# The seven column groups of the first batch, re-ordered: an FFT filter and a feed-forward block in one kernel

## The chip, the cores and the metric

The kernel runs on one core of one Trainium2 chip. Its engines are TensorE (PE in the profile, with its weight loads as PEld), VectorE (DVE), ScalarE (ACT), GpSimd (POOL) and SyncE (SP). SP, ACT and POOL each have a queue from which they issue transfers (DMAs); an issue that has to wait for data holds up everything behind it in that engine's queue. The metric is the device time of one execution in microseconds (us), lower is better.

## The reference

For each of 8 batches of 3008 rows by 256 columns, the rows are Fourier transformed, multiplied by a complex filter, and transformed back. The result goes through a feed-forward block of width 2048 with the activation h - tanh(h):

```python
X = np.fft.rfft(x, axis=1)
Y = X * (filt_r + 1j * filt_i)[None]
y = np.fft.irfft(Y, n=x.shape[1], axis=1)
h = y.reshape(-1, 256) @ w_in
out = (h - np.tanh(h)) @ w_out
```

Everything on TensorE is float32. The two weight matrices arrive as float64 and are converted to float32 on the chip.

## The kernel before, in words

The length 3008 is 64 times 47, and the transform is done in two steps each way. The first step (over 64) mixes the rows; the second (over 47, of which symmetry leaves 24) is done for 32 columns `a` of the first step. In batch 0 these 32 columns are worked in seven **column groups** (`SLOTS`): six of 5 columns, g = 0 to 5, with 5 times 24 = 120 partitions, and g = 6 with the last two columns, laid out at half width (two halves of 128 channels, one on top of the other).

The program has two parts. The **prologue** (from line 1101) works batch 0 up to the last step of its transform back; it also converts the first weights and takes the first columns of batch 1. The **main loop** (from line 1334) then runs over units `U`, four to each group of 4 output rows: `up` multiplies by w_in, `shrink` applies the activation, `down` multiplies by w_out, and the later batches' transforms are worked in between. The order of the instructions on each engine is the order in which the Python code emits them (`tc.manual_schedule()`): nothing reorders them.

In the prologue the loop over g (line 1208) emits for each group:

- `filters_of(g + 2)`, L1062: the filter rows of the group after next, loaded into one of three tiles, on SP for g above 1. Group 6 needs in addition a row that is zeroed (L1066), rows that `turned_rows` has brought into the DRAM tensor `filt` (read at L1067), and a shift of the upper half of the channels to the lower partitions by `under` (L1059, issue L1060);
- `across(g + 2)`, L1041: eight transposes on TensorE (L1050) and two copies by ACT into `a2`;
- `there0(g + 1)`, which is `forth`, L403: the second step of the transform for group g + 1. For each of two halves, two matmuls go to a bank (L411). ACT copies the first bank to `xy` (L414); VectorE forms sum and difference with the second (L416, L417) when the group's turn comes;
- `convert(3)`: three steps of the conversion of weights (`converted`, L169; ACT's step L180, VectorE's L182 to L200; seven steps a job, five jobs in the prologue). After the loop `convert(100)` does what is left;
- `filtered(g)`, L420: the complex product, L428 to L435 on VectorE and a last sum L437 on GpSimd, or on VectorE for g = 0, 5 and 6;
- `way_back()`: the transform back of the group before, `back0` (L1080): eight matmuls (L1087, L1089), two ACT copies (L1092) and two writes to the DRAM tensor `ct2` (L1093), on GpSimd's queue for g up to 4 and ACT's for g = 5. Group 6 has `back` (L446, L459).

`turned_rows` (L527) loads a filter row, negates it (L540), writes it to the DRAM tensor `less` (L541) and copies it turned round from there to `filt` (L531). The read waits for the write to land. Both are on GpSimd's queue, and in the loop they come at g = 2 in one piece, followed by the first two loads of the weights that the main loop converts (`begun`, L174).

After the loop, `rest` (L1073) reads the finished `ct2` back as `e2` in eight transfers on SP (L1077): four for the groups 0 to 4, and, behind the last way back, four for the groups 5 and 6. Then `first1` (L1170) takes the first eight columns of batch 1 (tile `x1`, loaded at g = 3; L1175), and `warmer(14)` (L1034) runs 14 matmuls whose result nobody reads. The main loop's first instruction on TensorE is `pu` (L576), which reads `e2`.

At the other end, `shrink` of the last unit but one ends with `combine` (L597 to L600: three differences and a fourth built on them) on VectorE, `down` of the last unit forms seven products (L787) and sums them (L801 to L821, two of the sums on GpSimd), and `store_last` (L877) transposes the result, copies it out of PSUM and sends it in two transfers, one each on SP and ACT.

The lists of steps that the two parts of the loop go by:

```python
steps_at = ([1, 1, 1, 1, 0, 1, 1, 0] if U > 1 else [0, 0, 1, 0, 2, 0, 2, 1])
...
chain = filtered(g, xy, fts.pop(g), V, V if g in (0, last_g - 1, last_g) else G, pro)
```

## Time and profile before

| | |
|---|---|
| runs, median (lowest to highest of 3) | 2564.8 us (2563.4 to 2569.96) |
| the profiled execution | 2566.24 us, span 2564.4 us |
| TensorE busy | 2540.9 us (99%) |
| VectorE busy | 1878.4 us (73%) |
| ScalarE busy | 1666.3 us (65%) |
| GpSimd busy | 1481.4 us (58%) |
| mean transfer rate | 83 GB/s, 212.43 MB in all |

The span is what the profiler saw between the first and the last instruction; the execution's own time is 1.8 us longer. All positions below are in microseconds from the span's start. A timeline row gives start, duration, engine, line, operation, what it writes and reads, its shape and how many instructions were merged into it, and in square brackets the idle time of the engine before it and what ended it. A float32 matmul stands in the trace as two records, so `x16` is eight matmuls. A row of the windows gives for each engine the busy time and the number of instructions in that stretch, then TensorE's granted clock (1.00 is full), the share of the DMA engines and what they moved. In a row of busy time and waits, the arrow `<-` ahead of an engine's name says what ended the wait.

### The profile page before, as it was taken

The page shows a single profiled execution, that of the slowest core. Times are in us where ns is not written, and L with a number is a line of the kernel's source. Part 1 is how long each engine was busy: PE and PEld are TensorE (multiplying, and loading weights), DVE is VectorE, ACT ScalarE, POOL GpSimd, SP SyncE. Part 2 cuts the span into 40 slices and gives each one's busy share as a digit, 9 for nine tenths or more (in the row PEclk, how much of TensorE's full clock was granted, in tenths as well). Part 3 has the DMA queues.
Part 4 walks back from the last instruction along what each step waited for, and adds up shares of the span by engine and source line. Part 5 has one row for each costly group of instructions (what it writes and reads, how often), then busy time and mean ns, then how long its engine had stood idle before and what let it go on. Part 6 is the DMA issues. An engine that isn't in the chain of part 4 may idle for free.

```text
span 2564.4 us, 44624 instructions
## 1 busy us (share of the span) xinstructions
PE 2540.9 (99%) x17076; PEld 2177.8 (85%) x17076; DVE 1878.4 (73%) x2265; ACT 1666.3 (65%) x2497; POOL 1481.4 (58%) x1124
## 2 busy tenths in 40 slices
PE   8999999999999999999999999999999999999998
PEld 7678888888898888988888888898889888898887
DVE  6788776887678876788668886688866877555555
ACT  4566666666666666666666666676666666666665
POOL 4256665666466655666656665566645666555552
PEclk9999999999999999999999999999999999999999
DMA  8873214422343323342233322443123322110110
GB/s 221 260 198 103 65 35 109 119 67 48 76 118 93 80 54 94 82 108 67 72 94 90 92 67 61 101 105 97 36 64 88 93 66 52 26 32 18 26 21 19
DMA packets 333660, 212.43 MB, mean 83 GB/s; under 512 B 231737, under 2 KB 304855, under 8 KB 329789
## 3 DMA queue, kind: packets, MB, share of 16 engines
q1 hardware_dynamic: 318511, 184.59, 29.5%
q0 software_dynamic: 11424, 17.03, 2.4%
q10 hardware_dynamic: 3502, 7.87, 0.9%
q8 instruction: 136, 2.23, 0.4%
q14 instruction: 87, 0.71, 0.1%
HBM read 128.75 MB, written 83.39 MB: 83 GB/s over the span
## 4 chain that ended last, share of the span: by engine, by line
PE 94%; DMA 2%; DVE 1%; ACT 1%; issue 1%; POOL 0%; ACTq 0%; POOLq 0%; DVEq 0%
PE o L787 43%; PE x L617 25%; PE z L617 12%; PE y L617 6%; PE pm L401 3%; PE pu L576 2%; DMA ct<-a 1%; PE pm L340 1%; DMA raw<-in_moe_w_in_dram 0%; DMA fh<-f 0%; DMA mats_sb<-mats 0%; PE pe L1089 0%; PE o L842 0%; PE pf L297 0%; PE warm L1038 0%
## 5 line engine op out<-in xcount | busy, mean ns | idle before, releaser
L787 PE MATMUL o<-t,wd 128*128 128x256 f32 (+1 forms) x3008 | 763.6, 377 | 0.0
L597 POOL TENSOR_TENSOR t<-h 128x512 f32<-128x512 f32 (+1 forms) x186 | 305.7, 1643 | 712.4 <-DVE h L739 703.9
L739 DVE TENSOR_TENSOR h<-h,y 128x1024 f32<-128x1024 f32 (+1 forms) x384 | 579.8, 1510 | 160.8 <-ACT y L735 157.3
L787 PEld LDWEIGHTS o<-t,wd 128*128 128x128 f32 x3008 | 569.3, 190 | 85.3 <-POOL o L815 15.1
L617 PE MATMUL x<-tu,wu 128*128 128x256 f32 (+1 forms) x2256 | 576.2, 378 | 0.2 <-ACT u L623 0.2
L787 PE MATMUL o<-h,wd 128*128 128x256 f32 (+1 forms) x2256 | 573.6, 377 | 1.8 <-DVE h L739 1.8
L787 PEld LDWEIGHTS o<-h,wd 128*128 128x128 f32 x2256 | 426.0, 190 | 72.8 <-issue 18.4
L623 ACT COPY s<-x 128x512 f32<-128x512 f32 (+1 forms) x188 | 108.6, 578 | 564.6 <-PE x L617 564.6
L617 PEld LDWEIGHTS x<-tu,wu 128*128 128x128 f32 x2256 | 423.6, 190 | 57.2 <-issue 3.7
L732 ACT ACTIVATE y<-y 128x1024 f32<-128x1024 f32 (+1 forms) x384 | 399.4, 1040 | 12.1
L735 ACT ACTIVATE y<-y 128x1024 f32<-128x1024 f32 (+1 forms) x384 | 399.8, 1041 | 4.6
L729 ACT ACTIVATE y<-h 128x1024 f32<-128x1024 f32 (+1 forms) x384 | 400.5, 1043 | 3.6 <-DVE h L665 1.7
L598 POOL TENSOR_TENSOR t<-h,t 128x512 f32<-128x512 f32 (+1 forms) x186 | 313.9, 1688 | 14.6
L600 POOL TENSOR_TENSOR t<-h,t 128x512 f32<-128x512 f32 (+1 forms) x186 | 303.7, 1633 | 0.0
L599 POOL TENSOR_TENSOR t<-h 128x512 f32<-128x512 f32 (+1 forms) x186 | 289.7, 1557 | 0.0
L623 ACT COPY u<-x 128x512 f32<-128x512 f32 (+1 forms) x376 | 213.3, 567 | 57.0 <-PE x L617 53.7
L665 DVE COPY h<-x 128x512 f32<-128x512 f32 (+1 forms) x188 | 127.8, 680 | 127.2 <-PE x L617 127.1
L617 PE MATMUL z<-tu,wu 128*128 128x256 f32 (+1 forms) x752 | 190.2, 376 | 0.4 <-DVE h L673 0.4
L617 PE MATMUL z<-ut,wu 128*128 128x256 f32 (+1 forms) x752 | 190.2, 376 | 0.4 <-DVE h L657 0.4
L617 PE MATMUL y<-ut,wu 128*128 128x256 f32 (+1 forms) x752 | 190.2, 376 | 0.0
L617 PE MATMUL x<-ut,wu 128*128 128x256 f32 (+1 forms) x752 | 190.2, 376 | 0.0
L657 DVE TENSOR_TENSOR h<-z,u 128x512 f32<-128x512 f32 (+1 forms) x188 | 127.2, 677 | 72.1 <-ACT u L623 71.1
(198 smaller groups left out, 2815.7 us busy)
## 6 DMA issues: line engine op xcount, KB each, us to landing
ft<-filt SPq DMA_DIRECT2D x28, 1024.0 KB
ct<-nn SPq DMA_DIRECT2D x56, 512.0 KB
e<-ct SPq DMA_DIRECT2D x47, 512.0 KB
a<-ct SPq DMA_DIRECT2D x112, 192.0 KB
out_dram<-ot SPq DMA_DIRECT2D x1248, 16.0 KB
x_sb<-in_x_dram SPq DMA_DIRECT2D x110, 128.0 KB
ct<-a SPq DMA_DIRECT2D x60, 128.0 KB
ct<-x_sb SPq DMA_DIRECT2D x60, 128.0 KB
```

The lines of the kernel that those rows point to most:

```text
L597: by.tensor_sub(t[0], b[0][1], b[0][0])
L598: by.tensor_sub(t[1], b[1][1], t[0])
L599: by.tensor_sub(t[2], b[1][1], b[0][1])
L600: by.tensor_sub(t[3], b[1][0], t[1])
L617: nc.tensor.matmul(bank[:, k], wu[:, q - 1, (2 * u + k) * 128:(2 * u + k + 1) * 128], rhs[q - 1], start=(first and k == 0), stop=True, ski ...
L623: ACT.copy(t, X)
L665: V.tensor_copy(h[:, 2, :, 0:w], X)
L729: ACT.activation(y[k], ht[k], AF.Arctan, scale=TURN)
L732: ACT.activation(y[k], y[k], AF.Tanh, scale=BEND)
L735: ACT.activation(y[k], y[k], AF.Square, scale=SCALE, accum_out=y_sums[:, 2 * U + k // 2:2 * U + k // 2 + 1])
L739: V.tensor_mul(ht[k], ht[k], y[k])
L787: nc.tensor.matmul(product(q), wd[:, q - 1, (2 * u + k) * 128: (2 * u + k + 1) * 128], rhs[q - 1][:, k], start=(u == 0 and k == 0 and q == ...
```

## The change

- `turned_rows`: the negation moves to GpSimd, and a `yield` splits the write to `less` from the copy that reads it. The write is emitted at g = 1, ahead of that group's way back, the copy at g = 2.
- The loads of the first two of the main loop's weights are emitted at g = 3 instead of g = 2, both on GpSimd's queue.
- `across(g + 2)` comes ahead of `filters_of(g + 2)`; group 6's zeroing moves from VectorE to GpSimd; the load of `x1` moves from g = 3 to the start of g = 2, and `first1` is made only where it is used.
- Group 5 (the sixth) forms its sums on TensorE: `forth(..., whole=True)` runs two matmuls into each result, so eight for four, and ACT copies both banks.
- Conversion steps in the loop: 3, 3, 3, 1, 0, 0 for g = 0 to 5, instead of 3 for each. From the third job on, the next job's ACT step is emitted after a job's third step.
- At g = 5 the way back of group 4 comes behind `there0(6)`, and no conversion stands there.
- The first four reads of `rest` go on GpSimd's queue.
- `warmer(14)` becomes `warmer(8)`.
- The tail: in the last unit but one a `yield` ahead of `combine`, and one more step at the end of `up`; the last `down` has its products in another order and one sum on VectorE instead of GpSimd; `store_last` works in two halves of two output columns each, with four transfers.

```diff
             for n, _ in enumerate(began[k]):
                 yield
-                if after and n == 2 and k + 1 < len(jobs):
+                if (after or k > 1) and n == 2 and k + 1 < len(jobs):
                     next(began[k + 1])
...
             for k in range(2):
-                nc.tensor.matmul(pa[:, k], way[2 * v + k], at[0:n, PLACE[2 * v + k], 0:w],
-                                 start=True, stop=True)
-            if v:
-                ACT.copy(xy[:, 2:4], pa)
+                if whole:
+                    nc.tensor.matmul(pa[:, k], way[k], at[0:n, PLACE[k], 0:w],
+                                     start=True, stop=False)
+                nc.tensor.matmul(pa[:, k], way[(3 - k if v else 2 + k) if whole else 2 * v + k],
+                                 at[0:n, PLACE[2 + k if whole else 2 * v + k], 0:w],
+                                 start=not whole, stop=True)
+            if v or whole:
+                ACT.copy(xy[:, 2 * v:2 * v + 2], pa)
             yield xy
-        V.tensor_add(xy[:, 0:2], pa, xy[:, 2:4])
-        V.tensor_sub(xy[:, 2:4], pa, xy[:, 2:4])
+        if not whole:
+            V.tensor_add(xy[:, 0:2], pa, xy[:, 2:4])
+            V.tensor_sub(xy[:, 2:4], pa, xy[:, 2:4])
...
-        V.tensor_scalar(out=t, in0=t, scalar1=-1.0, scalar2=None, op0=ALU.mult)
+        G.tensor_scalar(out=t, in0=t, scalar1=-1.0, scalar2=None, op0=ALU.mult)
         G.dma_start(dram(less_d, 0, [[DM, NH], [1, DM]]), t)
+        yield
         turned_to(1, less_d, NH - 1)
...
-        steps_at = ([1, 1, 1, 1, 0, 1, 1, 0] if U > 1 else [0, 0, 1, 0, 2, 0, 2, 1])
+        steps_at = ([1, 1, 1, 1, 0, 1, 1, 1] if U > 1 else [0, 0, 1, 0, 2, 0, 2, 1])
...
+        if U + 2 == 4 * len(groups):
+            yield
         combine(blocks, [t[:, k, :, 0:w] for k in range(4)],
...
-        mm(1, 2)
-        yield
-        if done:
+        last_unit = U + 1 == 4 * len(groups)
+        mm(*((2, 3) if last_unit else (1, 2)))
+        yield
+        if done and not last_unit:
             ACT.copy(p1, product(1))
             V.tensor_add(o[:, 0, 0:w], product(2), p1)
         yield
-        mm(3, 5)
-        yield
+        mm(*((1, 5) if last_unit else (3, 5)))
+        yield
+        if last_unit:
+            ACT.copy(p1, product(1))
+            V.tensor_add(o[:, 0, 0:w], product(2), p1)
...
-            G.tensor_add(x12, u2, x12)
+            (V if last_unit else G).tensor_add(x12, u2, x12)
+            if last_unit:
+                G.tensor_add(o[:, 1, w:2 * w], p1, p5)
...
-        for h, copy in ((0, ACT.copy), (1, V.tensor_copy)):
-            pt = psl([128, CH, 128], "xy"[h])
-            for j in range(CH):
-                nc.tensor.transpose(pt[:, j], o[:, h, j * 128:(j + 1) * 128], one)
-            copy(ot[:, :, h * 128:(h + 1) * 128], pt)
-        for (r, step, m, j, half), queue in zip(runs(c), (nc.sync, ACT)):
+        for lo, tag, copy in ((2, "x", ACT.copy), (0, "y", V.tensor_copy)):
+            pt = psl([128, 2, DM], tag)
+            for h in range(2):
+                for j in range(2):
+                    nc.tensor.transpose(pt[:, j, h * 128:(h + 1) * 128],
+                                        o[:, h, (lo + j) * 128:(lo + j + 1) * 128], one)
+            copy(ot[:, lo:lo + 2], pt)
...
                 if g == len(SLOTS) - 1:
-                    V.memset(t[0:1, 2:4], 0.0)
+                    G.memset(t[0:1, 2:4], 0.0)
...
             for g in range(last_g + 1):
+                if g == 2:
+                    x1 = load_x(big([128, 8, DM], F32, "x1"), 1, 0, 8)
                 if g + 2 <= last_g:
+                    a2[g + 2] = across(g + 2)
                     fts[g + 2] = filters_of(g + 2)
-                    a2[g + 2] = across(g + 2)
                 if g == 3:
                     e2s[0] = load_e2(0, 0, ())
-                    ones_1 = first1(load_x(big([128, 8, DM], F32, "x1"), 1, 0, 8))
                 if g == last_g - 1:
                     under(fts[last_g])
-                    convert(3)
-                    way_back()
                 if g < last_g:
                     there[g + 1] = there0(g + 1)
+                if g == last_g - 1:
+                    way_back()
                 next(there[g][0])
-                if g < last_g - 1:
-                    convert(3)
+                if g < last_g - 2:
+                    convert(3 if g < 3 else 1)
...
+                if g == 1:
+                    next(turning)
                 if g not in (0, last_g - 1):
                     way_back()
                 if g == 2:
                     next(turning)
+                if g == 3:
                     ahead = [begun(tiles1, job, queue=G) for job in jobs[5:7]]
-            rest(0, SG * (last_g - 1), [nc.sync])
+            rest(0, SG * (last_g - 1), [G])
...
-            warmer(14)
+            warmer(8)
```

More of the change, by code (lines that the diff above doesn't have):

```diff
@@ L401, in packed, with forth @@
             nc.tensor.matmul(to, weights_of, at, start=True, stop=True)
-    def forth(g, at, z):
+    def forth(g, at, z, whole=False):
         n, w = extent(g)
@@ L820, in down @@
             V.tensor_add(o[:, 1, 0:w], product(4), p1)
-            G.tensor_add(o[:, 1, w:2 * w], p1, p5)
+            if not last_unit:
+                G.tensor_add(o[:, 1, w:2 * w], p1, p5)
             accs.pop(i)
@@ L881, in store_last @@
         ot = dn.tile([128, CH, DM], F32, tag="ot", bufs=1, name="ot")
-        for h, copy in ((0, ACT.copy), (1, V.tensor_copy)):
-            pt = psl([128, CH, 128], "xy"[h])
-            for j in range(CH):
-                nc.tensor.transpose(pt[:, j], o[:, h, j * 128:(j + 1) * 128], one)
-            copy(ot[:, :, h * 128:(h + 1) * 128], pt)
-        for (r, step, m, j, half), queue in zip(runs(c), (nc.sync, ACT)):
-            queue.dma_start(dram(out.tensor, (b * SEQ + r) * DM,
-                                 [[NR * DM, 64], [step * DM, m], [1, DM]]),
-                            ot[64 * half:64 * half + 64, j:j + m])
+        for lo, tag, copy in ((2, "x", ACT.copy), (0, "y", V.tensor_copy)):
[5 more added lines that the diff above has]
+            copy(ot[:, lo:lo + 2], pt)
+            for (r, step, m, j, half), queue in zip(runs(c), (nc.sync, ACT)):
+                queue.dma_start(dram(out.tensor, (b * SEQ + r + step * lo) * DM,
+                                     [[NR * DM, 64], [step * DM, 2], [1, DM]]),
+                                ot[64 * half:64 * half + 64, j + lo:j + lo + 2])
     def store_some(n):
@@ L1191, in there0 @@
             def there0(g):
-                there = forth(g, a2.pop(g), z0)
+                there = forth(g, a2.pop(g), z0, g == last_g - 1)
                 xy = next(there)
@@ L1245 @@
             next(late)
-            for _ in ones_1:
+            for _ in first1(x1):
                 pass
-            warmer(14)
+            warmer(8)
         with tc.tile_pool(name="dn", bufs=2) as dn, \
```

## The prediction

> **What bounds the kernel now.** I read the page first, for who is busy, then the windows and the timeline of the first 90 us, where most of the diff works, then the end.
>
> ```profile
> span 2564.4 us, 44624 instructions
> ...
> PE 2540.9 (99%) x17076; PEld 2177.8 (85%) x17076; DVE 1878.4 (73%) x2265; ACT 1666.3 (65%) x2497; POOL 1481.4 (58%) x1124
> ```
>
> TensorE (PE) is busy for all but 23.5 us of the span. So only three things can shorten the kernel: less PE idle time, PE work taken out, or PE work that runs faster. The windows show the third: one record of the stage before the first unit is cheap or dear according to the granted clock.
>
> ```profile
> core 0: us, PE busy (x) PEld busy (x) DVE busy (x) ACT busy (x) POOL busy (x), PEclk, DMA share, GB/s
> 22.25:50.63 28.38, 26.26 (x144) 21.77 (x145) 25.43 (x39) 13.86 (x26) 12.79 (x18) 1.00 0.78 211
> ...
> 57.22:63.33 6.11, 6.11 (x14) 4.68 (x15) 4.23 (x6) 1.15 (x2) 3.61 (x4) 0.50 0.75 252
> 63.33:69.59 6.26, 4.49 (x25) 3.76 (x24) 4.70 (x7) 2.58 (x5) 3.14 (x5) 1.00 0.65 165
> 69.59:77.83 8.24, 7.67 (x24) 5.77 (x25) 7.78 (x16) 1.17 (x2) 0.50 (x1) 0.59 0.71 218
> ```
>
> In 57.22 to 63.33 and again after 69.59 the clock (the number before the DMA share) is at half. The timeline of PE says what came before:
>
> ```profile
> 50.63 1.03 PE L411 MATMUL pa<-a,mats_sb 120*120 120x256 f32 x4
> ...
> 57.22 1.21 PE L1089 MATMUL pe<-nn,mats_sb 120*120 120x256 f32 x2 [4.26 <-POOL nn L437]
> ...
> 69.59 0.67 PE L1087 MATMUL pe<-nn,mats_sb 120*120 120x256 f32 x2 [1.77 <-DVE nn L434]
> 70.83 1.21 PE L1089 MATMUL pe<-nn,mats_sb 120*120 120x256 f32 x2 [0.57 <-DVE nn L437]
> ...
> 76.95 1.05 PE L459 MATMUL pe<-xy,mats_sb 96*96 96x128 f32 x8
> 77.83 3.62 PE L1175 MATMUL pf<-x,f 128*128 128x256 f32 x16
> 81.29 6.21 PE L1038 MATMUL warm<-f 128*128 128x256 f32 x28
> 87.60 1.27 PE L576 MATMUL pu<-gt,e 64*64 64x64 f32 x64
> ```
>
> At full clock, 16 records of 256 columns take 81.29 - 77.83 = 3.46 us from start to start, so 0.216 us each (a matmul is two records). Groups are numbered g = 0 to 6. From 50.63 to 87.60 PE had this to do: group 5's way there 1.73 (8 records), three ways back of 16 records 10.38 (g = 3, 4, 5), group 6 there and back 0.88 each (8 records of 128 columns: 77.83 - 76.95), batch 1's first columns 3.46, 28 warming records 6.05. That is 23.4 us of work in 36.97 us: 13.6 us were lost there, half in gaps, half to the slow clock.
>
> The first gap hangs on GpSimd's queue (POOL), and what follows on SyncE's (SP):
>
> ```profile
> 48.02 0.55 POOL L541 DMA_DIRECT2D less<-neg  x1
> 53.73 0.68 POOL L531 DMA_DIRECT2D filt<-less  x1 [5.17 <-DMA less<-neg]
> ...
> 55.88 1.29 POOL L437 TENSOR_TENSOR nn<-nn,xy 120x512 f32<-120x512 f32 x1
> 57.94 0.34 SPq L1067 DMA_DIRECT2D filt<-filt  x1
> 64.20 0.64 SPq L1060 DMA_DIRECT2D filt<-filt  x1
> ```
>
> POOL writes the negated row to DRAM and stands 5.17 us until it has landed, because its next transfer reads it. Behind it in the queue are two weight loads and group 3's sum (L437), which the way back waits for.
>
> **The change, part by part.**
>
> *Row copies split.* The negation moves to POOL and the write goes out one group earlier, behind group 1's sum, so near 41; the read stays behind group 2's transfers, so at 48.02, where the write was. The landing took 53.45 - 48.02 = 5.4 us, so it is over by 46.5 and POOL does not stand. The two weight loads behind it go one group later. Group 3's sum then starts when DVE has its products. DVE's rows, and one of ACT's copies:
>
> ```profile
> 38.81 0.69 DVE L416 TENSOR_TENSOR xy<-pb,xy 120x512 f32<-120x512 f32 x1
> 41.96 1.22 DVE L428 TENSOR_TENSOR nn<-xy,filt 120x1024 f32<-120x1024 f32 x1
> 45.15 0.28 DVE L540 TENSOR_SCALAR neg<-neg 24x256 f32<-24x256 f32 x1
> ...
> 47.80 0.47 DVE L182 TENSOR_SCALAR top<-top 128x512 f32<-128x512 f32 x1 [1.05 <-ACT top L180]
> ...
> 71.59 0.69 DVE L428 TENSOR_TENSOR nn<-xy,filt 96x512 f32<-96x512 f32 x1
> ...
> 74.36 0.41 DVE L440 TENSOR_TENSOR xy<-nn 96x256 f32<-96x256 f32 x1
> ...
> 80.57 0.43 DVE L182 TENSOR_SCALAR top<-top 128x512 f32<-128x512 f32 x1 [2.82 <-ACT top L180]
> 83.41 0.69 DVE L200 TENSOR_TENSOR wu<-top,low 128x512 f32<-128x512 f32 x1
> ```
> ```profile
> L1092 ACT COPY e<-pe x6: 585/585/586, 60.2 to 77.2; 120x512 f32<-120x512 f32 x6
> ```
>
> A group's products take 45.15 - 41.96 = 3.19 us, its two sums twice 0.69. Without conversion steps between, group 3 ends on DVE at 45.2 + 1.4 + 3.2 = 49.8, group 4 at 54.4. POOL's sum of 1.29 follows, so group 3's is there by 51.3, group 4's by 56.1. On POOL the negation costs something no row shows: at least DVE's 0.28, at most L437's 1.29, which has ten times the elements; I take the lower half, 0.6, since it delays a transfer with 1.5 us in hand. The memset moved to POOL is of that kind and lies before group 4's sum: up to 0.6, in hand.
>
> *Sixth group's sums on TensorE.* 8 records more on PE, +1.73 us, which nothing hides since PE is the bound; one more ACT copy (0.59); two DVE sums (1.38) less. PE: 50.63 + 3.46 = 54.1; back of group 3 to 57.55 (sum there at 51.3); group 6 there to 58.4; back of group 4 to 61.9 (sum at 56.1); back of group 5 to 65.3; back of group 6 to 66.2. Group 5's products start when ACT has copied, at 54.8, and end with their sum at 58.7: 3.2 us ahead of need.
>
> *Group 6's filter rows.* They wait for the row written at 48.0. From that transfer's issue in the old run (53.73) to the first read (57.94) is 4.2 us, from there to the shift of the second half (64.20) 6.3 us, in which SP also sent the other shift, now ahead of it. So the new shift leaves at 58.5, lands some 2 to 2.5 us later at 61, and DVE then takes 74.77 - 71.59 = 3.2 us for the half-width group: 64.2, with PE asking at 65.3. Cover 1.1 us; if it is gone, each further us is a us lost.
>
> *Batch 1's columns earlier, and the order across / filter reads.* Three transfers of 1 MB move up one group on SP, ahead of group 4's rows. Those rows are wanted at 51.1, eight us after they were issued. I cost this at nothing; if the cover goes, the price is the delay of one filter landing, 0 to 2 us.
>
> *One conversion behind.* 8 of 23 steps leave the group loop, of which DVE steps were in its way. Behind the groups DVE now has three jobs of 84.1 - 80.57 = 3.5 us: 64.3 + 10.5 = 74.8, and ACT's step of the next job now comes ahead (the 2.82 us wait goes). Its next work for the units waits for pu and an ACT copy: 73.1 + 1.3 + 0.6 = 75.0. Hidden, by 0.2; bounds 0 to 1 us lost.
>
> *Warmer 14 to 8, and the reads behind.* 12 records less: PE reaches pu at 66.2 + 3.46 + 3.46 = 73.1, against 87.60: **14.5 us earlier**. Does the data come by then?
>
> ```profile
> 67.91 0.73 POOL L1093 DMA_DIRECT2D ct<-e  x1 [1.00 <-ACT xy L414]
> 69.26 3.02 SPq L1077 DMA_DIRECT2D e<-ct  x4
> 78.55 1.21 SPq L464 DMA_DIRECT2D ct<-e  x2
> 80.71 1.58 SPq L1077 DMA_DIRECT2D e<-ct  x4
> DMA to landing us min/median/max: 3.0/3.4/5.4
> ```
>
> The last four reads (SP) are out 80.71 + 1.58 - 77.83 = 4.5 us after the last way back; their landing is not shown. The write before them let the first go after 2.16 us (78.55 to 80.71); the tile's transfers took 3.0 to 5.4. With 2.2 from the issue the data is there 6.5 us after the way back, with 3.4 it is 7.7, and the shorter warming gives 6.9. I take 2.2, the row of the same size of transfer, so no wait; the other end costs 0.8.
> The first four go to POOL: behind group 4's last write (PE 61.9, ACT 0.6, issue 62.6, landing 3.4: 66.0) come three issues of 0.73, the last starting at 67.5, landing 3.0 to 5.4 later: 70.5 to 72.9. Just inside 73.1.
>
> *New tail.*
>
> ```profile
> 2540.22 0.69 DVE L597 TENSOR_TENSOR t<-h 128x512 f32<-128x512 f32 x1
> ...
> 2542.23 0.19 ACT L735 ACTIVATION_READ_ACCUMULATOR y<-y 128x1 f32 x1
> 2542.76 0.68 DVE L673 TENSOR_TENSOR h<-z,u 128x512 f32<-128x512 f32 x1
> ...
> 2543.48 1.06 ACT L729 ACTIVATE y<-h 128x1024 f32<-128x1024 f32 x1 [1.06 <-DVE h L673]
> 2548.11 2.02 PEld L787 LDWEIGHTS o<-h,wd 128*128 128x128 f32 x10 [1.97 <-DVE h L739]
> 2557.09 0.50 SPq L888 DMA_DIRECT2D out_dram<-ot  x1
> ```
>
> The yield puts L673 ahead of the four combining steps; ACT then goes on at 2542.42 instead of 2543.48, and the last units' chain up to 2548.11 comes 1.06 us earlier. The combined operands come 0.7 later, to records that run 1 us or more after. Then the reordered sums: x12 on DVE instead of POOL, and the output in two halves, the last issue within 0.2 us of where it was but with half the bytes. From 2557.09 to the span's end are 7.3 us, of which only moving bytes can shrink: 0 to 1.5 saved, -0.2 if the issues count; I take 0.5. **Tail: 1.5 us.**
>
> Sum: -14.5 - 1.5 = -16.0 on the profiled execution of 2566.24 us (span 2564.4, 1.8 around it). That execution is 1.4 above the median of 2564.8, so 2564.8 - 16.0 = **2548.8 us**. Behind pu PE stays the bound in the same order, so the gain should not be given back.
>
> **The rivals.**
> (1) *The reads come late.* If one of the eight lands 2 us after 73.1, PE waits 2 and may pay the slow clock again: the two gaps of 1.77 and 0.57 were followed by half clock, 14 records in 6.1 instead of 3.0 us. That is 3.1 + 2 = 5.1: 2554. For it: the landings above leave 0.2 to 0.4 us. Against: the median landing leaves 2. The page "SBUF — State Buffer" of the Trainium skill (Who interferes with whom) says that transfers issued by GpSimd starve while DVE runs a two-port step such as a tensor_scalar, which is what stands behind the groups here; here POOL's issue at 48.02, beside the step of 47.80 and the next, took 0.55, so nothing of it shows. The page "TensorE: Matmul & The Clock Gate" of the Trainium skill (Part 1) lets the clock fall only after an idle window of about 3.4 us; the row at 70.83 fell with less, so the measurement decides, and by the page this rival would be 2551.
> (2) *The group loop gets a new gap.* Filter rows or a POOL sum are late by 2 us and the clock falls once: again 5.1, 2554; by both gaps 2559, no measurable change. For it: 1.1 us of cover. Against: all other steps have 2 to 5.
> (3) *Slower: the transfers become the bound.* The three windows after 57.22 moved 212 GB/s on average; from 46 to 87.6 that is 8.8 MB, of which the 1 MB of batch 1 goes ahead: 7.8 MB. About 2.5 MB of it (the next batches' rows, two weight loads) is not waited for at pu, and 5.3 MB in the 27 us left ask for 196 GB/s. But all transfers share the engines: if all 7.8 MB must pass first, the kernel is slower than before below 7.8 / 43.1 = 181 GB/s, and at the lowest window, 165, it takes 47.3 us: pu at 93.3, 2564.8 + 5.7 - 1.5 = 2569.0. Against: at 165 the engines were busy for 0.65 only, and at 0.75 they moved 252.
> (4) *The stall only moves*, POOL still standing at the row copy: it would need a landing of over 10 us, twice the row's: about 2554, by one fall of the clock.
>
> **How the numbers follow.** Forecast 0.75 (2546 to 2552: the tail and read bounds, and 2 us of scatter of medians). Rival 1 0.10 and rival 2 0.09 (2551 to 2559), rival 3 0.04, rival 4 0.02. What a measurement can tell is 0.3%, 7.7 us, so faster means below 2557.1: 0.75 + 0.10 + a third of rival 2 = 0.88; same, the rest of rival 2 and rival 4, 0.08; slower 0.04. The range of 2545 to 2556 takes in the forecast and most of rivals 1 and 2.
>
> **What would show it.** Right: POOL without a wait at L531, granted clock 1.00 from 22 us to pu, PE without a gap over 1.2 us, back of group 6 near 66, pu near 73, PE's wait at the last L739 under 0.8. Wrong: a gap at pu ended by a read, half clock in any window, or a PE wait for L437, L416 or L440.

## The result and the profile after

| | before | after |
|---|---|---|
| median of 8 runs each | 2565.86 us (2563.4 to 2569.96) | 2558.34 us (2556.2 to 2562.93) |
| the profiled execution | 2566.24 us, span 2564.4 | 2556.2 us, span 2554.4 |

The ratio is 0.997, with an interval of 0.9959 to 0.9981: 7.5 us faster, where 16 were forecast, and the time lies outside the range of 2545 to 2556. The profiled pair differs by 10.0 us; the profiled execution of after was the fastest of its eight, 2.1 us under their median. Timed once more, beside new runs of before:

> The changed kernel once more. If its median holds: 2557 to 2559.5, 6 to 8 us below before, with the profiled execution not above the median; the ratio's interval then stays clear of the 0.9938 that 16 us would be. If the first eight runs were high by chance: 2554 to 2556.5.

2558.95 us (2558.16 to 2564.47, 11 runs) beside 2564.88 (25 runs), ratio 0.9979 (0.997 to 0.9988). The result stands.

First the timeline of PE after, from group 5's way there to the first unit:

```profile
51.16 0.60 PE L412 MATMUL pa<-a,mats_sb 120*120 120x256 f32 x2
...
65.42 0.59 PE L1106 MATMUL pe<-nn,mats_sb 120*120 120x256 f32 x2
68.45 1.76 PE L464 MATMUL pe<-xy,mats_sb 96*96 96x128 f32 x8 [2.44 <-DVE xy L444]
70.01 4.66 PE L1192 MATMUL pf<-x,f 128*128 128x256 f32 x16
74.51 3.62 PE L1055 MATMUL warm<-f 128*128 128x256 f32 x16
78.23 0.33 PE L582 MATMUL pu<-gt,e 64*64 64x64 f32 x4
79.00 1.15 PE L582 MATMUL pu<-gt,e 64*64 64x64 f32 x60 [0.44 <-DMA e<-ct]
```

The first 14.7 us went as forecast: no gap, and the back of group 5 ends at 65.85 (65.3 was forecast). Then comes what was forecast not to come: 2.44 us without work, and after it dear records. Group 6's way back took 1.56 us from start to start (68.45 to 70.01; 0.88 before) and batch 1's first columns 4.50 (3.46). pu starts at 79.0 instead of 73.1. The windows give the clock beside it:

```profile
core 0: us, PE busy (x) PEld busy (x) DVE busy (x) ACT busy (x) POOL busy (x), PEclk, DMA share, GB/s
51.16:58.07 6.91, 6.91 (x35) 5.84 (x33) 6.38 (x7) 2.66 (x5) 5.94 (x8) 1.00 0.88 244
58.07:65.85 7.78, 7.78 (x41) 6.55 (x39) 3.36 (x7) 2.61 (x5) 2.86 (x5) 1.00 0.70 220
65.85:71.00 5.15, 2.71 (x12) 2.39 (x12) 4.88 (x12) 1.32 (x3) 3.08 (x6) 0.78 0.76 193
71.00:75.20 4.20, 4.20 (x19) 3.57 (x18) 4.00 (x8) 2.73 (x5) 0.00 (x0) 0.87 0.93 332
```

The clock (the number ahead of the DMA share) is 1.00 up to the gap, and then 0.78 and 0.87 on average.

What L464 waited for is the product with the filter rows, and those hang on transfers. DVE's timeline shows the wait of this product (L433 of group 6):

```profile
65.47 0.69 DVE L433 TENSOR_TENSOR nn<-xy,filt 96x512 f32<-96x512 f32 x1 [4.32 <-DMA filt<-filt]
```

The chain of the work that ended last, in order of time (start, duration, what):

```profile
57.91 4.07 DMA filt<-in_filt_i_dram
...
62.26 3.03 DMA filt<-filt
...
69.80 5.35 DMA ct<-e
...
76.31 2.45 DMA e<-ct
```

And the queues of POOL and SP, from the timeline of after:

```profile
42.05 0.60 POOL L546 DMA_DIRECT2D less<-neg  x1 [0.29 <-POOL neg L545]
48.53 0.69 POOL L536 DMA_DIRECT2D filt<-less  x1
53.27 0.74 POOL L174 DMA_DIRECT2D ft<-in_moe_w_in_dram  x1
54.01 0.74 POOL L174 DMA_DIRECT2D ft<-in_moe_w_out_dram  x1
...
55.55 2.62 SPq L1087 DMA_DIRECT2D filt<-in_filt_i_dram  x4
62.26 0.66 SPq L1077 DMA_DIRECT2D filt<-filt  x1
...
68.58 0.75 POOL L174 DMA_DIRECT2D a<-in_moe_w_out_dram  x1
69.32 0.75 POOL L174 DMA_DIRECT2D a<-in_moe_w_in_dram  x1
69.79 1.34 SPq L469 DMA_DIRECT2D ct<-e  x2
75.22 1.37 SPq L1094 DMA_DIRECT2D e<-ct  x4
```

POOL no longer stands at L536. But twice two weight loads of 512 KB each go out within a microsecond or two of small transfers that something waits for: at 53.27 and 54.01 beside group 6's last filter rows, and at 68.58 and 69.32 just ahead of the last write of `ct`. That write let the first read go after 5.43 us (69.79 to 75.22) instead of 2.16. In the timeline of before the same loads went out at almost the same times:

```profile
54.40 0.74 POOL L174 DMA_DIRECT2D ft<-in_moe_w_in_dram  x1
...
68.63 0.75 POOL L174 DMA_DIRECT2D a<-in_moe_w_out_dram  x1
```

There the first pair was 3.5 us ahead of group 6's rows, which began at 57.94, and the second 9.9 us ahead of the last write at 78.55. It is the small transfers that have moved up to the loads: the rows now begin at 53.0, the write at 69.79.

The 10.0 us of the profiled pair: 8.7 up to pu's end (88.87 to 80.15) and 1.3 behind it. Behind pu, a new wait of 0.74 for an ACT copy takes 0.5 away (before had one of 0.23), 0.4 lies in smaller differences, and the tail brings 1.4: PE's waits for the last products (us in total, times, the longest) were these in before and after:

```profile
PE o L787 <- DVE h L739: 1.8, 2, 1.6
```
```profile
PE o L795 <- DVE h L745: 0.2, 1, 0.2
```

The 5.9 us that pu is later than forecast: 0.55 from the work up to the back of group 5, 2.6 from there to L464, 1.7 from the half clock, 0.3 in the warming, and 0.8 at pu, where four records ran at 78.23 and the others waited for the last reads.

One pair of executions says only so much. The run t1 below has the prologue of before unchanged, and its pu begins at 85.31, 2.3 us earlier than in the profiled execution of before. So a part of the 8.7 us is this one execution's late pu.

### The profile page after: what moved, and what is told of

Read it like the earlier page. It is cut to its first block, busy times and chain, and to the rows that moved or that the text cites. A ratio compares the mean times of both kernels' runs of the same rounds, so it can differ in the third digit from the quotient of the medians.

```text
span 2554.4 us, 44623 instructions
## 1 busy us (share of the span) xinstructions
PE 2535.7 (99%) x17072; PEld 2173.1 (85%) x17072; DVE 1875.8 (73%) x2262; ACT 1667.1 (65%) x2498; POOL 1484.3 (58%) x1129
## 4 chain that ended last, share of the span: by engine, by line
PE 94%; DMA 3%; DVE 1%; ACT 1%; issue 0%; SPq 0%; POOL 0%; ACTq 0%; POOLq 0%; DVEq 0%
PE o L795 44%; PE x L623 25%; PE z L623 12%; PE y L623 6%; PE pm L401 3%; PE pu L582 2%; DMA x<-in_x_dram 1%; PE pm L340 1%; DMA filt<-in_filt_r_dram 1%; DMA ct<-a 0%; PE o L857 0%; PE pf L297 0%; DMA filt<-filt 0%; DMA ct<-e 0%; DVE wd L231 0%
```

## The experiments

Two theories for the late transfers. **A**: the weight loads on GpSimd's queue stand ahead of the small transfers, in DMA engines that all queues share. **B**: the small transfers take that long by themselves, or by the queue on which they are issued. And a question of its own: is what is won at pu kept to the end?

The table gives each run's positions in its trace. "Shift" is the issue of group 6's last half-row shift, "write to read" the time from the issue of the last write of `ct` to that of the first read behind it, "pu" the start of its long run, "rest" what lies from pu's end to the end of the span. A time without a count of runs is one execution.

| kernel | shift | write to read | pu | rest | time (runs) |
|---|---|---|---|---|---|
| before | 64.20 | 2.16 | 87.60 | 2475.5 | 2565.86 (8) |
| after | 62.26 | 5.43 | 79.00 | 2474.2 | 2558.34 (8) |
| after_again | 62.61 | 5.38 | 78.98 | 2476.6 | 2558.95 (11) |
| e1_all_loads_behind | 58.21 | 4.38 | 75.47 | 2480.9 | 2559.79 (10) |
| e2_first_two_early | 62.12 | 3.85 | 79.81 | 2476.3 | 2559.91 |
| e3_last_two_behind | 61.98 | 2.42 | 77.66 | 2474.7 | 2555.48 |
| e3_again | 62.05 | 2.34 | 77.94 | 2481.3 | 2559.68 (9) |
| e4_rest_on_sp | 61.58 | 5.58 | 78.08 | 2475.9 | 2557.39 |
| u1_copies_together | 64.52 | 3.67 | 82.53 | 2476.5 | 2562.14 |
| u2_sums_on_vector | 62.46 | 3.73 | 79.95 | 2477.6 | 2560.62 |
| c1_two_more_loads | 64.45 | 4.23 | 81.80 | 2473.2 | 2558.27 |
| b1_rows_first | 62.74 | 2.96 | 78.68 | 2474.5 | 2558.91 (10) |
| b2_first_two_at_five | 58.79 | 8.79 | 79.88 | 2474.6 | 2561.87 (10) |
| b3_x1_late | 59.05 | 4.39 | 77.63 | 2480.6 | 2559.7 (9) |
| b4_front_loaded | 64.12 | 2.81 | 78.21 | 2481.6 | 2563.33 (10) |
| w1_warm_14 | 63.02 | 5.20 | 83.32 | 2475.9 | 2562.39 |
| s1_split_alone | 65.65 | 7.07 | 84.55 | 2477.2 | 2565.85 (10) |
| t1_tail_alone | 64.71 | 3.83 | 85.31 | 2474.8 | 2563.26 |

### All four loads behind the last reads

```diff
-                if g == 3:
-                    ahead = [begun(tiles1, job, queue=G) for job in jobs[5:7]]
...
             convert(100)
+            behind = cst.tile([32, 1], F32, name="behind")
+            G.tensor_copy(behind, e2s[0][0][96:128, 0, 0:1])
+            ahead = [begun(tiles1, job, queue=G) for job in jobs[5:7]]
```

> From the changed kernel; all four weight loads of 512 KB that stood on GpSimd's queue in the prologue (issued at 53.3, 54.0, 68.6 and 69.3) wait until the last read of e2 has landed. Theory A (bulk loads stand ahead of the small transfers in the DMA engines): group 6's shift is issued by 60 instead of 62.3 and lands by 63 instead of 65.4; TensorE's wait of 2.4 us before the last way back goes; from the last ct2 write to the first read 2 to 3 us instead of 5.4; pu starts between 73 and 75.5 instead of 79.0; time 3 to 5 us below the changed kernel. Theory B (the small transfers take that long by themselves): shift, reads and pu stay within 0.7 us of where they were, the time is the same or, because the weights come later, up to 3 us longer.

The timeline of PE and SP in this run, and two rows of its list of waits (waiting engine, what ended the wait; us in total, times, the longest):

```profile
58.21 0.65 SPq L1077 DMA_DIRECT2D filt<-filt  x1
65.06 1.04 PE L464 MATMUL pe<-xy,mats_sb 96*96 96x128 f32 x8
66.65 1.62 SPq L469 DMA_DIRECT2D ct<-e  x2
71.03 1.53 SPq L1094 DMA_DIRECT2D e<-ct  x4
...
ACT xy L180 <- DMA ft<-in_moe_w_in_dram: 6.4, 1, 6.4
ACT a L299 <- DMA ct<-a: 6.5, 4, 3.2
```

Without the loads the shift leaves at 58.21, the 58.5 that was forecast, and the way back of group 6 starts with no wait at full clock. That is A for the first place. At the second place only part went: 4.4 us instead of 5.4. pu comes 3.5 us earlier, yet the time is 2559.79 (ratio to before 0.9978, 0.9969 to 0.9988), no better than after: the rest is 6.6 us longer than in after, and 4.3 longer than in after_again. ACT now waits for the weights (the first row), which costs PE one wait of 1.2 us at 87.73; PE's other waits there, 1.1 to 1.4 us each, are for ACT's copies L299, which wait for writes to `ct` (the second row).

### Only the first two loads early, only the last two behind

```diff
+                if g == 1:
+                    ahead = [begun(tiles1, job, queue=G) for job in jobs[5:7]]
                 if g == 2:
                     next(turning)
-                if g == 3:
-                    ahead = [begun(tiles1, job, queue=G) for job in jobs[5:7]]
```

> From the changed kernel; only the first two weight loads move, from g = 3 to g = 1, so near 44 instead of 53.3, well ahead of group 6's filter rows. Theory A: the shift lands 1.5 to 2.5 us earlier than 65.4, the wait before the last way back falls under 1 us, and the last writes, still beside the second pair of loads, take 4 us or more to the first read. Theory B: the shift lands at 65.4 within 0.7.

The pair now goes out at 45.1, ahead of the copy from `less`, and that copy of 24 KB takes 7.2 us (4.5 in after): I read this as the loads delaying another transfer. The shift stays at 62.12. A had it 1.5 to 2.5 us earlier and missed; by the shift alone this run would fit B, and it is the run above, with the loads gone, that speaks against B.

The other pair (the two lines of `behind` alone):

> From the changed kernel; only the third and fourth weight load (68.6 and 69.3) wait until e2 has landed. Theory A: the shift stays at 62.3 and 65.4, TensorE still waits 2.4 us for it, but from the last ct2 write to the first read it is 2 to 3 us instead of 5.4, and pu no longer waits for a read: 78.2 instead of 79.0, as the matmuls without a use end there. Theory B: 5 us to the first read as before.

```profile
69.55 1.48 SPq L469 DMA_DIRECT2D ct<-e  x2
71.97 1.50 SPq L1094 DMA_DIRECT2D e<-ct  x4
...
77.66 1.38 PE L582 MATMUL pu<-gt,e 64*64 64x64 f32 x64
```

These rows of its timeline show 2.4 us from write to read, and pu without a wait right behind the warming: A, for the second place, whole.

### The first reads on SP's queue

```diff
-            rest(0, SG * (last_g - 1), [G])
+            rest(0, SG * (last_g - 1), [nc.sync])
```

> From the changed kernel; the first four reads of e2 go back to SP's queue. Theory A: the queue makes no difference to the last writes, which stand behind the weight loads; those are issued some 3 us earlier on GpSimd's queue, so the last writes meet less of them and the first read behind them comes 3 to 5 us after the write. Theory B in its form that the reads on GpSimd's queue are the delay: the first of the last reads comes 2.2 us after the write and pu does not wait for data.

Write to read stays at 5.58 us, and pu waits 2.28 us for the last reads. The queue on which the reads are issued makes no difference, so B in its queue form falls at this place; in its other form it fell with the run before. A's number, 3 to 5 us, missed too: the loads went out 6.0 us ahead of the write and cost as much as those 1.2 us ahead of it in after. What size the delay takes is not explained. The Trainium skill's page "DMA: Bandwidth & Descriptors" (Issuing engines are not separate DMA queues) says that transfers started by different engines run interleaved on the same DMA engines; these runs agree.

### More load, less load, another order

```diff
                     ahead = [begun(tiles1, job, queue=G) for job in jobs[5:7]]
+                    for k in range(2):
+                        G.dma_start(wu[:, 3 * k:3 * k + 3, 768:1024],
+                                    dram(x.tensor, (5 + k) * SEQ * DM, ...))
```

> From the changed kernel; two further loads of 0.39 MB each, whose data is overwritten later and used by nobody, stand on GpSimd's queue right behind the first two weight loads (so near 54.7 to 56.2). Theory A (bulk loads ahead of small transfers): the shift is issued 2 to 3.5 us later than 62.3 and the last way back starts 2 to 4 us later than 68.45. Theory B (the small transfers' own time): both within 0.7 us, as GpSimd's other work has over 1 us in hand.

Two loads of 0.39 MB more at 53.9: the shift leaves 2.2 us later, group 6's way back starts 2.7 later, pu 2.8. Its one time, 2558.27, is still like after's.

With the first pair moved behind group 6's rows (`if g == 5` for `if g == 3`) and the last pair behind the reads:

> From the changed kernel; the first two weight loads go to the end of g = 5 (GpSimd near 64.5, behind group 4's writes), past group 6's filter rows, and the third and fourth behind e2. Theory A: group 6's rows behave as in the run with all loads behind (shift issued near 58.2, no wait before the last way back, which starts near 65.1); the last writes at 66.7 now meet the first pair, so 4 to 6 us to the first read and e2 near 76; pu near 76.5; the weights land by 72, ahead of their use near 78, so the units don't lose what the run with all loads behind lost. Time 1.5 to 3 us below the changed kernel. Theory B: no change of the shift, time within 1 us.

```profile
65.82 1.04 PE L464 MATMUL pe<-xy,mats_sb 96*96 96x128 f32 x8
...
79.88 2.56 PE L582 MATMUL pu<-gt,e 64*64 64x64 f32 x64 [6.11 <-DMA e<-ct]
```

Its timeline has the shift at 58.79 and no gap at L464, but the pair, now at 64.2 and 65.0, meets the last write at 67.41: 8.8 us to the read, and pu waits 6.1. A had given 4 to 6 us for that read. What was won at one place went at the next. 2561.87, ratio 0.9987 (0.9978 to 0.9997).

With group 6's plain rows ahead of the turned ones, and the last pair behind:

> From the changed kernel, two edits: group 6's eight plain filter rows are sent ahead of the read that waits for the turned row, so from 51.5 instead of 53.5 and mostly ahead of the two weight loads at 53.3; and the third and fourth weight load wait for e2, as in the run that moved these alone. Theory A: the shift is issued by 60.5, the wait before the last way back falls from 2.4 to under 0.8 with full clock, the last way back starts by 66.8, the first read comes 2 to 3 us after the write, pu starts by 75.5 and the time is 2.5 to 4 us below the changed kernel, as the first pair of weights still comes early for the units. Theory B: the rows' own landing sets the shift, which moves by the 2 us of the earlier issue at most and not by more than 0.7 if the read of the turned row is the last to land.

The last transfer is issued at 56.89 and has landed only at 62.7. A had given 60.5, so that number missed, and so did its pu of 75.5 (78.68 came); a shift within 0.7 us of after's is what B gave. Sending the rows earlier alone doesn't help; that the loads at 52.7 and 53.4 hold up the last of them is the reading that fits the runs without these loads. 2558.91 (ratio 0.998, 0.997 to 0.999), no different from after.

### Single parts of the change

The split alone, put into the kernel before:

```diff
-        V.tensor_scalar(out=t, in0=t, scalar1=-1.0, scalar2=None, op0=ALU.mult)
+        G.tensor_scalar(out=t, in0=t, scalar1=-1.0, scalar2=None, op0=ALU.mult)
         G.dma_start(dram(less_d, 0, [[DM, NH], [1, DM]]), t)
+        yield
...
+                if g == 1:
+                    next(turning)
```

> From the kernel before; only the negation on GpSimd and the split of the row copies (write at g = 1, copy at g = 2) are put in, nothing else. Theory of the forecast (the stall and both half-clock stretches hang on this): GpSimd no longer waits at the copy, group 3's sum ends at 53.5 instead of 57.2, TensorE's gap of 4.3 us falls under 1, the clock stays full to 66, and VectorE, with all its conversion steps in the loop, ends group 6 near 69.6 instead of 74.8: last way back at 70 instead of 77, pu near 80.3, time 6 to 8 us below before. That would be nearly the whole measured gain of the change, with the rest of the edits worth 0 to 2 us as they stand. Rival (the order of the other edits is needed too): pu at 84 or later, gain under 4.

PE's timeline in this run:

```profile
53.72 0.69 PE L1090 MATMUL pe<-nn,mats_sb 120*120 120x256 f32 x2 [0.43 <-POOL nn L437]
...
58.83 0.66 PE L1088 MATMUL pe<-nn,mats_sb 120*120 120x256 f32 x2 [1.83 <-DVE nn L434]
...
61.06 1.21 PE L1090 MATMUL pe<-nn,mats_sb 120*120 120x256 f32 x2 [1.57 <-POOL nn L437]
```

The gap of 4.26 us is gone, and others of 1.83 and 1.57 take its place, since the conversion steps still stand in VectorE's way. pu comes 3.0 us earlier than in before, but only 0.8 earlier than in t1, whose prologue is unchanged, and the time doesn't move: 2565.85, ratio 1.0002 (0.9992 to 1.0011). The forecast of 6 to 8 us missed, and the rival came true by its numbers: the split needs the order of the other edits.

The split undone in the changed kernel (`yield` and the call at g = 1 taken out):

> From the changed kernel; only the split is undone: negation, write to less and the copy that reads it stand together at g = 2 again, on GpSimd. Theory of the forecast (the stall hangs on this alone): GpSimd stands some 5 us ahead of the copy, so group 3's sum is done near 57 instead of 51.8 and TensorE, which asks for it at 55, waits about 2 us; the copy goes 6 us later, so group 6's filter rows, already the last to come, land near 71 instead of 65.4, the last way back starts near 74 with the clock at half, pu near 84, time 4 to 6 us above the changed kernel. Rival (the filter rows are late for other reasons, so the split is worth only the stall): shift at 66 or earlier, pu within 2 us of 79.

POOL stood for 2.24 us only, not 5, and group 3's sum still came in time. The price came by the filter rows: group 6's way back at 71.31 instead of 68.45, pu 3.5 later, 2562.14. The forecast's theory had both the stall and the later rows, and larger; the stall itself cost nothing. So the split is worth some 3.5 us at pu here (one execution), and alone no time at all.

The sixth group's sums left on VectorE:

> From the changed kernel; the sixth group's two sums go back to VectorE, so 8 records (1.73 us) less on TensorE and 1.4 us more on VectorE. If TensorE bounds this stage, as the forecast has it: the last way back starts 1.7 us earlier than 68.45 and pu 1.7 us earlier than 79.0. If group 6's filter rows bound it: TensorE waits about 4 us instead of 2.4 and the last way back stays at 68.5 within 0.5, pu within 0.7; the sums on TensorE are then neither gain nor loss.

```profile
68.78 1.99 PE L464 MATMUL pe<-xy,mats_sb 96*96 96x128 f32 x8 [4.72 <-DVE xy L444]
```

PE has 1.73 us less to do and waits 4.72 instead of 2.44 for the same rows. In after the matmuls added to PE lie in that wait.

Fourteen warming matmuls again (`warmer(14)`):

> From the changed kernel; the matmuls without a use are 14 again. They end 2.6 us later, at 80.7; since pu waits for e2 to 79.0 already, it starts 1.7 us later only, and with the clock kept up. The forecast priced this edit at 2.6 us.

pu is 4.3 us later: 2.6 of warming, 1.0 by a later way back of group 6 in this execution, 1.4 by a longer stretch at half clock, less the 0.8 that after waits at pu. The clock was not kept up, and the single time, 2562.39, can't be put down to the warming alone.

The tail alone, put into the kernel before (the parts of the diff in `shrink`, `down`, `store_last` and `steps_at`):

> From the kernel before; only the new tail is put in. The wait of 1.56 us before the last unit's first products falls under 0.3, the prologue is unchanged, and from those products to the end of the span it is 16.3 us as before (the halves of the output bring nothing): 1.3 us in all, which a single time can't tell from its scatter; the rows can. Rival, the forecast's: 0.5 us more at the end, so 15.8 from those products on.

The wait at the last products falls to 0.2 there as well. From the last unit's first products to the end of the span it is 15.99 us here, 16.28 in before, 16.39 in after and 16.40 in after_again: the output in halves brought 0.3 us in this one execution and nothing in the changed kernel.

### Is the gain at pu kept?

The first pair far ahead of the groups, x1's load behind the shift, the last pair behind the reads; and the same with x1 left where it was:

```diff
             next(turning)
+            ahead = [begun(tiles1, job, queue=G) for job in jobs[5:7]]
...
-                if g == 2:
-                    x1 = load_x(big([128, 8, DM], F32, "x1"), 1, 0, 8)
...
                     under(fts[last_g])
+                    x1 = load_x(big([128, 8, DM], F32, "x1"), 1, 0, 8)
```

> From the changed kernel; the first two weight loads go ahead of the group loop (GpSimd near 33), batch 1's columns (1 MB) go to SP behind group 6's shift (near 59), the third and fourth weight load behind e2. Theory A with the gain kept: shift issued near 58.5, last way back near 65.5 with full clock, first read 2.5 to 4 us after the last write, pu at 74 to 76 (TensorE may wait up to 1 us for batch 1's columns), and since the first weights are there from the start, the units lose no more than in the changed kernel: time 3 to 5 us below it. Rival, the gain is lost in the units whatever is done: pu as early, but from pu to the end 3 us or more longer than the 2475 of the changed kernel, median within 1.5 us of it.

> From the changed kernel; as the run with batch 1's columns late, but these stay at g = 2 (near 36), so 1 MB of weights and 1 MB of columns both pass between 33 and 46, where the engines' share was 0.92 already. Theory A: now the transfers of the early groups are the late ones: the write to less, the filter rows of groups 4 and 5 and the copy land 1 to 4 us later, and TensorE gets a wait of 1 us or more before 58; pu no earlier than 77. If the early transfers have room after all: pu at 74 to 76 as in the other run.

In b3 the shift leaves at 59.05 and group 6's way back starts without a wait, as A had it, but pu begins at 77.63 (its first four records at 77.05), not at 74 to 76: 1.4 us earlier than after, with a rest 6.4 longer (2559.7, ratio 0.9976, 0.9966 to 0.9986). In b4 the early transfers are the late ones, as A had it there: POOL stands 3.14 us at the copy from `less`, PE waits 1.5 us at 46 and again at 60, and the shift leaves at 64.12; the rest is 7.4 longer (2563.33, ratio 0.9991, 0.9982 to 1.0). PE's rows in b3's timeline and in b4's:

```profile
101.50 3.38 PE L297 MATMUL pf<-x_sb,f 128*128 128x256 f32 x8 [3.56 <-ACT a L299]
```
```profile
103.93 3.48 PE L297 MATMUL pf<-x_sb,f 128*128 128x256 f32 x8 [3.83 <-DMA x_sb<-in_x_dram]
```

In b4 PE waits for batch 1's later columns themselves; in b3 for an ACT copy, which in its own row waits for a write to `ct`. The eight records that cost 1.89 us at full clock then cost 3.4 to 3.5. Last, e3 once more, with more runs:

> The changed kernel with only the last two weight loads put behind the landing of the last reads, once more and timed. In the one look its first read followed the last write by 2.4 us instead of 5.4, pu started at 77.66 instead of 79.00, and the span was 2553.7 instead of 2554.4. If the loads in front of the last transfers cost what pu shows, and nothing gives it back, the median is 1 to 2 us below the changed kernel's 2558.3 to 2559.0: 2556.5 to 2558. If what is won at pu is lost at later transfers, as in the runs with the first two loads moved, the median is 2558.3 to 2560, and the stretch from the end of pu to the end of the span is longer than 2475.

2559.68 us (2554.74 to 2566.83, 9 runs), ratio 0.9976 (0.9966 to 0.9986). So e3 isn't better than after. Up to pu its two profiled executions go alike (77.66 and 77.94), and then this one loses 6.6 us. The first fence is the timeline of PE and the windows of e3_again, the second the windows of e3:

```profile
102.53 3.53 PE L297 MATMUL pf<-x_sb,f 128*128 128x256 f32 x8 [4.05 <-DMA x_sb<-in_x_dram]
147.79 1.13 PE L623 MATMUL x<-tu,wu 128*128 128x256 f32 x4 [2.08 <-ACT u L629]
...
80.00:120.00 40.00, 35.95 (x107) 21.06 (x106) 30.68 (x58) 23.84 (x41) 15.44 (x21) 0.96 1.06 298
```
```profile
80.00:120.00 40.00, 40.00 (x126) 23.58 (x125) 36.04 (x68) 27.58 (x47) 17.42 (x24) 1.00 1.04 328
```

The same instructions in the same order, the DMA engines full in both (1.06 and 1.04): in one the columns land in time, in the other 4 us late, with the fall of the clock on top. Before and after themselves have these engines as full, in the windows of the one and the other:

```profile
100.00:120.00 20.00, 20.00 (x65) 12.03 (x64) 17.26 (x30) 16.68 (x28) 10.66 (x16) 1.00 0.98 333
```
```profile
100.00:120.00 20.00, 20.00 (x63) 11.79 (x62) 19.35 (x39) 14.29 (x25) 11.77 (x16) 1.00 1.00 326
```

The loss has an end: from the run of pu that starts at 180 to 190 us, every kernel with the new tail takes 2371.8 to 2373.3 us to the end of the span. So whatever is won or lost behind the first pu lies ahead of that.

From here I infer that up to about 160 us the transfers are a second bound beside PE, so that an earlier pu starts to pay less than its own length. It wasn't tried with fewer bytes, which would be the direct proof.

## Why the prediction was wrong

**Held.** *Row copies split*: POOL passes L536 without a wait at 48.53, group 3's sum is there in time, PE is gapless at clock 1.00 from 51.16 to 65.85, 0.55 us later than worked out. The negation on POOL took 1.00 us (0.6 taken, 0.28 to 1.29 as bounds). *Sixth group's sums on TensorE*: the sum put down 1.73 us on the path; once the filter rows set the pace they cost nothing (u2). *One conversion behind* stayed hidden.

**Failed first: "Group 6's filter rows".** The step took two durations from before: 4.2 us from the copy's issue to the first read, 6.3 from there to the shift. The first held (48.53 to 53.0). The second became 9.3 (53.0 to 62.26): in before the two loads had 3.5 us of lead on the rows, now both go out together. I had counted the loads' new place only in POOL's queue ("one group later"), not in the DMA engines. With the loads gone the shift left at 58.21 (e1), with more of them at 64.45 (c1). The shift's own landing, put at 2 to 2.5 us with no row behind it, took 3.0 (62.26 to 65.29). Cost: 2.6 us of gap and 1.7 of half clock.

**Failed second: "Does the data come by then?"** The 2.16 us from write to read was measured 9.9 us behind the second pair of loads; the forecast moved the write up next to them and kept the duration. It took 5.43 us. e3, with the pair behind, brings back 2.4. That is not the whole of it: e1 and b3 took 4.4 with all four loads elsewhere, and why stays open. Cost at pu: 0.8 us, because the half clock had already made PE late.

**Rivals 1 and 2 came true together**, at 5.9 us of the 16. Their mechanism is rival 3's (all transfers share the engines), but what counted wasn't the bytes of the whole stretch: it was which bulk load stood ahead of which small transfer.

**Failed third: "the gain should not be given back".** In after's profiled execution it isn't (rest 2474.2, before 2475.5, of which the tail is 1.4). In after_again, close to the median, 2.3 us more are gone behind pu (rest 2476.6), with pu at the same place. And of the kernels that bring pu still earlier, e1, b3, b4 and one of e3's two executions lost 6 to 7.5 us behind it; e3's other execution, e4 and b1 (pu at 77.7 to 78.7) did not lose it. The median of after is 2.1 us over its profiled execution, which fits after_again's loss; the cause, late transfers, is inferred above and not shown. No kernel with repeated runs that brings the transfers at one or both places in time is faster than after (e1, b1, b2, b3, b4, e3_again: medians 2558.9 to 2563.3). So the two failed steps are shown for pu, and not for the total time.

***New tail***: 1.06 forecast for the chain, 1.4 measured (the longest wait from 1.6 to 0.2); 0.5 for the output in halves, nothing measured in the changed kernel. The last issue row of after reads 2.13 us for two transfers, from 2546.50, where before has 0.50 for one; whether the two further issues take the time that the smaller transfers save is not shown.

Sum: 16.0 forecast; minus 5.9 at pu and 0.1 in the tail gives the 10.0 of the profiled pair (the smaller differences above cancel); the last 2.5 to the medians' 7.5 are the two executions' places among their runs (before 0.4 over, after 2.1 under its median). So part of the 10.0 is luck. A second pair shows it: t1, with the old prologue, ends pu at 86.58 and after_again at 80.13, 6.5 us apart, and after_again loses 1.8 us of that behind pu; with the tail's 1.4, which both have, this makes 6.1. The 87.60 from which the forecast took its 14.5 us was itself a late pu, 2.3 us behind t1's.

## What to carry to other kernels

When a transfer is moved, look not only at the queue that it leaves but at every small transfer that will be in flight beside it at the new place: a write to DRAM and the read behind it took 3.7 to 8.8 us (5.4 in the changed kernel) with a megabyte of loads around it or up to 6 us ahead, and 2.2 to 4.4 where these loads stood elsewhere. A duration taken from the old trace holds only for the neighbours that it had there. And where the DMA engines are near full, a stage that ends earlier can move its stall to the next transfer, so judge such a change by the end of the span over several executions, not by the stage that was mended.

## What was not expected of the hardware

- **The clock after a gap.** In after and e3_again a gap of 2.44 us was followed by half clock within 0.6 us. In e4 a gap of 2.60 us was followed by full clock throughout (L464 1.09 us, the 16 records behind it in 3.45), and in b1 3.45 us, in after_again 2.92, by full clock for the eight records of L464 and then a fall. The length of the gap alone doesn't decide. The page "TensorE: Matmul & The Clock Gate" of the Trainium skill (Part 1) counts in free-running windows of about 3.4 us; that would let equal gaps end differently, but a whole idle window can't lie in 2.44 us, so the falls here say that less than that is enough.
- **A sum on POOL slows products on DVE.** A group's product, 1.22 us in the trace of before, took this in the timeline of after, while POOL's L442 ran from 55.23 to 56.49:

```profile
55.43 2.15 DVE L433 TENSOR_TENSOR nn<-xy,filt 120x1024 f32<-120x1024 f32 x1 [0.40 <-ACT xy L418]
```

  The page "SBUF — State Buffer" (Who interferes with whom) of the Trainium skill says that a VectorE instruction with two inputs in SBUF contends with a GpSimd instruction that reads SBUF; the row agrees. Its cost was hidden here.
- **Small work on POOL is dear**: the negation of 24x256 took 1.00 us there and 0.28 on VectorE.
